# Y W from thirds of the channels, on two halves of the array

## The chip, the cores and the metric

The kernel runs on one core of one Trainium2 chip. The metric is the device time of one execution in microseconds (us), the median over several runs.

## The reference

The input x has 8 batches, 3264 positions and 192 channels. Two operations follow each other.

```python
# 1. causal convolution of 7 taps; the taps of each of 8 heads go through a softmax
w = softmax(weight)                       # [8 heads, 7 taps]
x = sum over k of w[head, k] * x_padded[:, s + k, :]
# 2. spectral mix on 64 modes
X = rfft(x, axis=1)[:, :64]               # Xr, Xi
Yr = Xr w_r - Xi w_i                      # per mode a 192 x 192 matrix
Yi = Xr w_i + Xi w_r
y = irfft(Y, n=S)                         # the other modes are zero
u = x + y
out = u + relu(u @ w_ch)                  # w_ch is 192 x 192, called W below
```

The large inputs are x (20 MB), w_r and w_i (9.4 MB each); the output has 20 MB. All are float32; the kernel works in bfloat16 and accumulates in float32.

## The kernel before, in words

The core has five engines that run side by side, each in the order of its own instructions: TensorE (PE; the profile shows its loads of the stationary operand apart, as PEld), VectorE (DVE), ScalarE (ACT), GpSimd (POOL) and SyncE (SP). POOL issues nearly all DMAs, SP a few. The order on each engine is the order of the program text (a manual schedule); waits between engines are put in by the framework, from the parts of tiles that an instruction reads and writes.

Batches are handled in four pairs q = 0 to 3, positions in tiles t of 128 (25 whole ones and a half). A partition of the tile `xall` is a position; the two batches of a pair lie side by side.

**Convolution stage.** `units` are groups of 4 or 5 position tiles. Per unit, `conv` multiplies with a band matrix on 64 x 64 quarters of the array, and two casts write the result back into `xall`: channels 0 to 95 by ACT (L325) and 96 to 191 by DVE (L327). `dft_unit` accumulates the 64 modes, `xtrans` turns them so that channels lie on the partitions. `c_bank` transposes the convolved x into `cc`, with the channels split in thirds (channel 3p + j lies in partition p of third j). The loads of x (L151) are issued ahead, a few small ones among them by the table `beside`.

**Mix stage.** `load_w` (L428) loads the matrices of four modes per group g; `mix` (L439) multiplies them. The result of two groups, a pair d, is copied by ACT into `ymix` (L452), transposed by `mix_trans` (L459), and copied into `yet` (L466 on DVE, L468 on ACT). In `yet`, the partitions are 96 channels, in two halves t; the cosine and the sine part c lie side by side. `PLAN` spreads the waiting transposes (`some`) over the groups. The last group's second half goes through mix, copy and transposes by itself.

**End stage.** The output of a position tile is x W + (inverse transform of Y W) under the relu, plus the inverse transform of Y, plus x. So three kinds of products go into one accumulator: `c_part` (x W, L496, from `cc` and `wc`, two halves of 64 rows at the same time), `m_part(n, 0)` (L516, from Y W), then ACT's relu in place (`relu`, L547), then `m_part(n, 1)` (from Y), and `finish` (L572): DVE adds x into an output buffer and a DMA writes it. Items n are pairs of tiles, `duos`, in a list; the accumulators `zt` are four, so c_part(n + 4) waits for finish(n). The loop runs so, for each n: m_part(n, 0), relu(n), c_part(n + 1), m_part(n - 1, 1), finish(n - 1).

Y W and Y themselves come out of `zw_part` (L523), once for each pair q: for q = 0 before the loop, for q = 1, 2, 3 as items of the list at places 2, 8 and 11, where it uses the accumulator of its place. Item 14 (`"h"`) is the half tiles of all pairs. `zw_part` multiplies 96 rows (channels) of `yet` with `wm` and `w1`, which hold the two halves of the rows of W with an identity beside them, so that each product gives Y W and part of Y. Its result has four blocks of 96 columns; the inner two are Y W, the outer two Y (`QUARTERS`). `zw_copy` scales it into `zw`: DVE L530, ACT L528.

```python
for t, w in enumerate((wm, w1)):
    for i, r in enumerate(ROWS):
        nc.tensor.matmul(z[r, HD - HD * t:2 * D - HD * t], yet[0:HD, t, 2 * q + i, c, :], w[0:HD, :],
                         start=(t == 0), stop=(t == 1), tile_position=(0, 64 * i), skip_group_check=True)
```

The identities of `wm` and `w1` are made by POOL (L253, L254) between the loads of x, and their W is loaded by `small(0)` and `small(1)` (L227) behind the last matrices. `wc` is loaded by `small(2)` and `small(3)` (L229) among the loads of x.

Of the kernel before, what the change touches and what calls it, by code (L numbers as in the profile page):

```python
# [9 lines left out]
ALU = mybir.AluOpType  # L10
# [3 lines left out]
BF16 = mybir.dt.bfloat16  # L14
# [5 lines left out]
def kernel(  # L20
# [9 lines left out]
    nc = tc.nc  # L30
    B, S, D = x.shape
    H, KK = weight.shape
    MODES = moe_w_r.shape[0]
# [3 lines left out]
    P = 128  # L37
# [15 lines left out]
    def sb(name, shape, dtype, **kw):  # L53
        return pool.tile([P] + shape, dtype, tag=name, name=name, **kw)
# [4 lines left out]
    NW = 4  # L59
# [7 lines left out]
    fsin = sb("fsin", [NT, P], BF16)  # L67
    tabs = (ftab, fsin)

    HD = D // 2  # L70
    yet = sb("yet", [2, B, 2, MODES], BF16)

    mixa = sb("mixa", [3 * 2 * B * MODES], BF16)
    xt = mixa[:, :].rearrange("p (j k m) -> p j k m", j=3, k=2 * B)

    zw = mixa[:, 0:4 * NQ * D].rearrange("p (q c b e) -> p q c b e", q=NQ, c=2, b=4)
    QUARTERS = (slice(1, 3), slice(0, 4, 3))
    band = sb("band", [H, 2 * P], BF16)

    wm = sb("wm", [3 * HD], BF16)  # L80
    w1 = sb("w1", [3 * HD], BF16)
    wc = sb("wc", [3, D], BF16)
    ident = sb("ident", [P], BF16)
    perm = sb("perm", [P], BF16)
    ascale = sb("ascale", [1], F32)
# [136 lines left out]
                                     NT * (2 * g + 1):NT * (2 * g + 2) + 1:NT, 0, :], in_=src)  # L222

    def small(k):
        if k < 2:
            w, c, r = ((wm, 0, slice(HD, D)), (w1, HD, slice(0, HD)))[k]
            nc.gpsimd.dma_start(out=w[0:HD, c:c + D], in_=moe_w_ch[r, :])  # L227
        else:
            nc.gpsimd.dma_start(out=wc[64 * (k - 2):64 * (k - 2) + 64, :, :],  # L229
                                in_=moe_w_ch.rearrange("(p j) d -> p j d", j=3))  # L230

    beside = {3: (load_half, 0, 0), 4: (load_half, 0, 1), 6: (load_half, 1, 0), 7: (load_half, 1, 1),
              12: (small, 2), 15: (small, 3)}

    def load_units(k0, k1):
        for k in range(k0, k1):
# [12 lines left out]
    nc.gpsimd.affine_select(out=perm[:, 64:128], in_=perm[:, 64:128], compare_op=ALU.not_equal, fill=1.0,  # L249
                            base=0, pattern=[[-1, 64]], channel_multiplier=1)  # L250
    load_units(5, 9)
    for w, c in ((wm, D), (w1, 0)):
        nc.gpsimd.memset(w[0:HD, c:c + HD], 0.0)  # L253
        nc.gpsimd.affine_select(out=w[0:HD, c:c + HD], in_=w[0:HD, c:c + HD], compare_op=ALU.not_equal,  # L254
                                fill=1.0, base=0, pattern=[[-1, HD]], channel_multiplier=1)
    nc.gpsimd.memset(ascale[:], 2.0 / S)
    nc.gpsimd.memset(ascale[0:1, :], 1.0 / S)
    nc.gpsimd.memset(ascale[64:65, :], 1.0 / S)
# [8 lines left out]
                                                                  mybir.DependencyReason.DATA),  # L267
                              reason="row tiles take turns on a bank")

    LO, UP = slice(0, 64), slice(64, P)  # L270

    def conv_step(q, t0, n, half, step):

# [133 lines left out]
    for k, u in enumerate(units):  # L407
        conv(*u)
        if k < 2:
            table(*PARTS[k + 1])  # L410
        if waiting:
            xtrans(*waiting.pop(0), 0)
        if k:
            q, t0, n = units[k - 1]
            dft_unit(q, t0, n)
            if t0 + n == NT:
                waiting = [(q, 0), (q, 1)]
            if k > 1:
                some(XJOBS[k], min(NT * q + t0 + n, NT * (NQ - 1)))
# [14 lines left out]
    def mix(g):  # L434
        yp = low[(g // 2) % 2][:, D * (g % 2):D * (g % 2) + D]
        for j in range(3):
            for p4 in range(4):
                m = 4 * g + p4
                nc.tensor.matmul(yp[32 * p4:32 * p4 + 2 * B, :], xt[:, j, :, m],  # L439
                                 wbuf(g)[:, p4, j, :], start=(j == 0), stop=(j == 2),  # L440
                                 tile_position=(0, 32 * p4), skip_group_check=True)
        if g < NW:
            load_w(g + NW + NL)
        elif g >= NW + NL:
            load_w(g + NW)
            if g + NW == NG - 1:

                small(0)
                small(1)

    def mix_copy(d, gs=slice(0, 2)):
        nc.scalar.copy(out=ymix[d % 2][:, gs, :],  # L452
                       in_=low[d % 2][:, 0:2 * D].rearrange("p (g d) -> p g d", g=2)[:, gs, :])

    def mix_trans(d, gs=slice(0, 2)):
        ets = [low[2 + t][:, :].bitcast(BF16)[:, 0:2 * P].rearrange("p (g k) -> p g k", g=2) for t in range(2)]
        for t in range(2):
            for g in range(gs.start, gs.stop):
                nc.tensor.transpose(ets[t][0:HD, g, :], ymix[d % 2][:, g, HD - HD * t:D - HD * t], ident[:])  # L459
        m = slice(8 * d + 4 * gs.start, 8 * d + 4 * gs.stop)  # L460
        for t in range(2):
            dst = yet[0:HD, t, :, :, m].rearrange("p b c m -> p c b m")
            srcv = ets[t][0:HD, gs, :].rearrange("p g (q k) -> p (g q) k", q=4)[:, :, 0:16].rearrange(
                "p m (c b) -> p c b m", c=2)
            if t == 0:
                nc.vector.tensor_copy(out=dst, in_=srcv)  # L466
            else:
                nc.scalar.copy(out=dst, in_=srcv)  # L468
# [7 lines left out]

    ROWS = (LO, UP)

    def c_part(n, ks=(0, 1)):
        duo, zt = items[n]
        if duo[0] == "h":
            for a in range(2):
                for j in range(3):
                    for k in range(2):
                        for i, r in enumerate(ROWS):
                            h = ROWS[i ^ k]
                            nc.tensor.matmul(zt[h, k, D * a:D * a + D], cc[r, 2 * k + a, 3 * NF + j, h], wc[r, j, :],
                                             start=(a == 0 and j == 0), stop=False, skip_group_check=True,  # L490
                                             tile_position=(r.start, h.start))
            return
        for k, (q, t) in enumerate(duo):
            for j in range(3) if k in ks else ():
                for i, r in enumerate(ROWS):
                    nc.tensor.matmul(zt[:, i, D * k:D * k + D], cc[r, q, 3 * t + j, :], wc[r, j, :],  # L496
                                     start=(k == 0 and j == 0), stop=False, skip_group_check=True)

    def m_part(n, which):

        duo, zt = items[n]
        for c in range(2):
            end = which == 1 and c == 1
            if duo[0] == "h":
                for k in range(2):
                    for i, r in enumerate(ROWS):
                        h = ROWS[i ^ k]
                        nc.tensor.matmul(zt[h, k, 0:2 * D], tabs[c][r, NF, 0:HALF], zw[r, 2 * k:2 * k + 2, c, QUARTERS[which], :],
                                         start=False, stop=end, skip_group_check=True,
                                         tile_position=(r.start, h.start))  # L510
                continue
            (q0, t0), (q1, t1) = duo[0], duo[-1]
            parts = [(0, 2, q0, t0)] if t0 == t1 and q0 != q1 else [(k, 1, q, t) for k, (q, t) in enumerate(duo)]
            for k, w, q, t in parts:
                for i, r in enumerate(ROWS):
                    nc.tensor.matmul(zt[:, i, D * k:D * (k + w)], tabs[c][r, t, :], zw[r, q:q + w, c, QUARTERS[which], :],  # L516
                                     start=False, stop=end and k + w == len(duo), skip_group_check=True)

    def zw_part(q, c, z):

        for t, w in enumerate((wm, w1)):
            for i, r in enumerate(ROWS):
                nc.tensor.matmul(z[r, HD - HD * t:2 * D - HD * t], yet[0:HD, t, 2 * q + i, c, :], w[0:HD, :],  # L523
                                 start=(t == 0), stop=(t == 1), tile_position=(0, 64 * i), skip_group_check=True)

    def zw_copy(dst, src, act):
        if act:
            nc.scalar.activation(out=dst, in_=src, func=ACT.Copy, scale=ascale[:, 0:1])  # L528
        else:
            nc.vector.tensor_scalar(out=dst, in0=src, scalar1=ascale[:, 0:1], scalar2=None, op0=ALU.mult)  # L530
# [82 lines left out]
    c_part(0)  # L613
    mix_trans(NG // 2 - 1, slice(1, 2))
    c_part(1, (0,))
    for c in range(2):
        zw_part(0, c, low[2 * c])
    for w in QUARTERS:
        for c in range(2):
            zw_copy(zw[:, 0, c, w, :], low[2 * c][:, 0:2 * D].rearrange("p (b e) -> p b e", b=4)[:, w, :], c)  # L620
    c_part(1, (1,))
    low_stack.close()
    stack, pp = psum_pool("pz1", "right")
# [6 lines left out]
    for n in range(N + 1):  # L630
        if is_duo(n) and duos[n] != ("h",):
            m_part(n, 0)
            relu(n)
        if n + 1 < N and n > 0:
            if is_duo(n + 1):
                c_part(n + 1)
                if duos[n + 1] == ("h",):

                    m_part(n + 1, 0)
                    relu(n + 1)  # L640
            else:
                q, zt = items[n + 1]
                for c in range(2):
                    zw_part(q, c, zt[:, c, :])
                for act, w in enumerate(QUARTERS):
                    zw_copy(zw[:, q, :, w, :], zt[:, :, 0:2 * D].rearrange("p c (b e) -> p c b e", b=4)[:, :, w, :],
                            act)
        if is_duo(n - 1):
            m_part(n - 1, 1)
            finish(n - 1)  # L650
# [30 lines left out]
```

## Time and profile before

| | |
|---|---|
| median of 4 runs | 180.48 us (179.97 to 180.79) |
| the profiled execution | 180.16 us |
| its span, first to last instruction | 178.4 us |
| mean granted clock of TensorE | 0.983 of full |
| busy PE, DVE, ACT, POOL | 146.9, 113.0, 98.2, 100.5 us |
| HBM read, written | 39.40 MB, 20.05 MB |

The profile is of one execution. Times in it count from the first instruction of the span; the execution's own time is 1.76 us longer than the span. Busy time of PE includes the flight of pipelined products, so its busy time is not its full rate. A row of a group gives line, engine, operation, output and inputs with their shapes, the count, and durations; "idle before" names what ended the engine's wait, and "issue" stands for a wait for nothing that the profile shows.

### The profile page before, as it was taken

The numbers are of one execution on the slowest core, as the hardware profiler recorded it, in microseconds if no ns is written. First come the engines' busy times: TensorE is split into PE (matmuls) and PEld (weight loads), VectorE is DVE, ScalarE is ACT, GpSimd is POOL, SyncE is SP. The second block draws the span as 40 slices with busy tenths as digits, with TensorE's granted clock in tenths as the row PEclk, the third lists the DMA queues.
The fourth block names the chain that finished last, engine by engine and source line by source line (L and its number), as shares of the span: only waits on it lengthen the run. The fifth ranks groups of instructions, "written<-read, shape, count | busy, mean of one in ns | idle before, by whom it ended". The sixth has DMA issues, their size and how long they took to land.

```text
span 178.4 us, 6295 instructions
## 1 busy us (share of the span) xinstructions
PE 146.9 (82%) x2736; PEld 108.6 (61%) x2736; DVE 113.0 (63%) x161; ACT 98.2 (55%) x135; POOL 100.5 (56%) x155
## 2 busy tenths in 40 slices
PE   0047879999999998796767769999999999999940
PEld 0033456666666665674655656966778888888820
DVE  1878564766866683444435362695788888888870
ACT  8176645544554735163354555767566777666630
POOL 7999988868855644433336100035354766665770
PEclk9999999999999999789999999999999999999997
DMA  3999999999999999999999970567689899998895
GB/s 43 167 176 188 190 190 189 192 191 194 188 191 191 204 206 207 206 207 206 206 206 206 207 120 4 174 227 281 252 248 364 329 366 354 355 348 352 334 355 192
DMA packets 44331, 40.17 MB, mean 225 GB/s; under 512 B 28800, under 2 KB 40656, under 8 KB 44304
## 3 DMA queue, kind: packets, MB, share of 16 engines
q0 software_dynamic: 41136, 37.59, 105.8%
q1 hardware_dynamic: 3168, 2.19, 4.0%
q8 instruction: 21, 0.34, 0.8%
q14 instruction: 6, 0.05, 0.1%
HBM read 39.40 MB, written 20.05 MB: 333 GB/s over the span
## 4 chain that ended last, share of the span: by engine, by line
DMA 42%; POOL 31%; issue 14%; PE 8%; POOLq 1%; DVE 1%; DVEq 0%
DMA arena<-in_moe_w_i_dram 18%; DMA xall<-in_x_dram 18%; POOL out_dram L580 17%; POOL xall L151 10%; DMA cc<-in_moe_w_i_dram 7%; PE za L516 2%; PE za L496 2%; POOL arena L428 1%; PE zb L516 1%; PE zb L496 1%; POOL xall L221 1%; PE zb L523 1%; DVE arena L572 1%; PE low L439 1%; POOLq L676 0%
## 5 line engine op out<-in xcount | busy, mean ns | idle before, releaser
L580 POOL DMA_DIRECT2D out_dram<-arena x45 | 33.9, 754 | 39.6 <-DVE arena L572 38.6
L151 POOL DMA_DIRECT2D xall<-in_x_dram x48 | 38.6, 812 | 7.0 <-DMA xall<-in_x_dram 4.6
L307 PE MATMUL z<-xall,band 64*64 64x192 bf16 (+3 forms) x816 | 27.4, 264 | 14.5 <-ACT band L195 10.5
L327 DVE CAST xall<-z 128x768 bf16<-128x768 f32 (+1 forms) x24 | 24.5, 1021 | 13.9 <-PE z L307 12.5
L307 PEld LDWEIGHTS <-band 64*64 64x64 bf16 x816 | 18.4, 110 | 22.9 <-ACT band L195 10.9
L325 ACT CAST xall<-z 128x768 bf16<-128x768 f32 (+1 forms) x24 | 20.4, 850 | 20.6 <-PE z L307 19.8
L496 PEld LDWEIGHTS <-cc 64*128 64x128 bf16 x600 | 27.3, 94 | 6.1 <-issue 1.3
L572 DVE TENSOR_TENSOR arena<-za,xall 128x768 f32<-128x768 f32 x26 | 24.7, 956 | 5.3 <-ACT zb L547 2.0
L547 ACT ACTIVATE za<-za 128x768 f32<-128x768 f32 (+1 forms) x27 | 21.0, 783 | 8.5 <-PE za L516 8.4
L572 DVE TENSOR_TENSOR arena<-zb,xall 128x768 f32<-128x768 f32 x23 | 21.9, 956 | 5.0 <-ACT zb L547 1.7
L547 ACT ACTIVATE zb<-zb 128x768 f32<-128x768 f32 (+1 forms) x25 | 19.6, 782 | 9.2 <-PE zb L516 8.9
L333 PE MATMUL low<-xall,ftab 128*128 128x384 bf16 x100 | 22.0, 348 | 0.0
L387 PEld LDWEIGHTS <-xall 128*128 128x128 bf16 x300 | 18.5, 104 | 3.2 <-issue 0.3
L362 DVE COPY cc<-r 128x1024 bf16<-128x1024 bf16 (+1 forms) x16 | 10.2, 670 | 13.7 <-ACT xs L452 6.2
L516 PE MATMUL za<-mixa,ftab 64*128 64x384 bf16 (+1 forms) x120 | 18.2, 304 | 0.0
L516 PE MATMUL za<-mixa,fsin 64*128 64x384 bf16 (+1 forms) x120 | 18.2, 304 | 0.0
L496 PE MATMUL za<-wc,cc 64*128 64x192 bf16 x318 | 18.1, 243 | 0.0
L516 PE MATMUL zb<-mixa,ftab 64*128 64x384 bf16 (+1 forms) x100 | 16.2, 313 | 0.4 <-ACT zb L547 0.4
L516 PE MATMUL zb<-mixa,fsin 64*128 64x384 bf16 (+1 forms) x100 | 16.2, 313 | 0.0
L496 PE MATMUL zb<-wc,cc 64*128 64x192 bf16 x282 | 15.9, 243 | 0.1
L428 POOL DMA_DIRECT2D arena<-in_moe_w_r_dram x12 | 7.4, 615 | 13.7 <-PE low L439 8.5
L516 PEld LDWEIGHTS <-ftab 64*128 64x128 bf16 x220 | 12.0, 94 | 4.2 <-issue 2.0
(110 smaller groups left out, 185.9 us busy)
## 6 DMA issues: line engine op xcount, KB each, us to landing
out_dram<-arena POOLq DMA_DIRECT2D x45, 384.0 KB, 4.3
xall<-in_x_dram POOLq DMA_DIRECT2D x24, 192.0 KB, 7.4
xall<-in_x_dram POOLq DMA_DIRECT2D x16, 240.0 KB, 7.2
arena<-in_moe_w_r_dram POOLq DMA_DIRECT2D x12, 288.0 KB, 9.2
arena<-in_moe_w_i_dram POOLq DMA_DIRECT2D x12, 288.0 KB, 10.0
out_dram<-arena SPq DMA_DIRECT2D x9, 192.0 KB, 2.4
xall<-in_x_dram POOLq DMA_DIRECT2D x8, 144.0 KB, 7.1
cc<-in_moe_w_r_dram POOLq DMA_DIRECT2D x4, 288.0 KB, 11.6
```

What stands on the lines that cost most here:

```text
L151: nc.gpsimd.dma_start(out=xall[:, s0:s0 + nf, i, :], in_=src)
L307: mm = nc.tensor.matmul(ov[c], band[r, h, c.start + shift + 64 * (r is UP and c is LO): c.start + shift + 64 * (r is UP and c is LO) + 64] ...
L325: nc.scalar.copy(out=dst, in_=srcv)
L327: nc.vector.tensor_copy(out=dst, in_=srcv)
L333: nc.tensor.matmul(xp, ftab[:, t, :], xall[:, slot(q, t), :, :], start=(t == 0), stop=False, skip_group_check=True)
L362: nc.vector.tensor_copy(out=out, in_=in_)
L387: nc.tensor.transpose(tp[:, P * k:P * k + P], src, ident[:])
L496: nc.tensor.matmul(zt[:, i, D * k:D * k + D], cc[r, q, 3 * t + j, :], wc[r, j, :], start=(k == 0 and j == 0), stop=False, skip_group_check ...
L516: nc.tensor.matmul(zt[:, i, D * k:D * (k + w)], tabs[c][r, t, :], zw[r, q:q + w, c, QUARTERS[which], :], start=False, stop=end and k + w = ...
L547: nc.scalar.activation(out=zt[:, :, 0:w], in_=zt[:, :, 0:w], func=ACT.Relu)
L572: nc.vector.tensor_tensor(out=o[:, :, :].rearrange("p k (i d) -> p i k d", i=2), in0=zt[:, :, 0:2 * D].rearrange("p i (k d) -> p i k d", k=2),
L580: nc.gpsimd.dma_start(out=dst, in_=ov)
```

## The change

Y W and Y are now made from thirds of the channels. `mix_trans` transposes each third twice, once into partitions 0 to 63 and once into 64 to 127 (12 transposes of 64 columns for a pair, in one bank, in place of 4 of 96 in two). From the lower half DVE takes the cosine part, from the upper half ACT the sine part, so that `yet` has 64 channels of one third on each half. `zw_part` then multiplies the two halves of the array side by side, three products each, of 384, 320 and 256 columns, for both batches of the pair at once.

The moving operand is `wc`, as in the c products, widened by an identity for each third; `wm`, `w1`, their POOL instructions and their two loads go. The identity columns of `wc` are written by DVE, one memset and three additions, after the fourth unit of the convolution. Y comes out in the order of thirds, and the copy into `zw` puts it back in order. For pairs 2 and 3 both copies run on ACT; for pairs 0 and 1 they stay with DVE and ACT.

```diff
-    yet = sb("yet", [2, B, 2, MODES], BF16)
+    yet = sb("yet", [3, B, MODES], BF16)
...
-    wm = sb("wm", [3 * HD], BF16)
-    w1 = sb("w1", [3 * HD], BF16)
-    wc = sb("wc", [3, D], BF16)
+    wc = sb("wc", [3, 2 * D], BF16)
...
     def small(k):
-        if k < 2:
-            w, c, r = ((wm, 0, slice(HD, D)), (w1, HD, slice(0, HD)))[k]
-            nc.gpsimd.dma_start(out=w[0:HD, c:c + D], in_=moe_w_ch[r, :])
-        else:
-            nc.gpsimd.dma_start(out=wc[64 * (k - 2):64 * (k - 2) + 64, :, :],
-                                in_=moe_w_ch.rearrange("(p j) d -> p j d", j=3))
+        nc.gpsimd.dma_start(out=wc[64 * k:64 * k + 64, :, 0:D], in_=moe_w_ch.rearrange("(p j) d -> p j d", j=3))
...
-    for w, c in ((wm, D), (w1, 0)):
-        nc.gpsimd.memset(w[0:HD, c:c + HD], 0.0)
-        nc.gpsimd.affine_select(out=w[0:HD, c:c + HD], in_=w[0:HD, c:c + HD], compare_op=ALU.not_equal,
-                                fill=1.0, base=0, pattern=[[-1, HD]], channel_multiplier=1)
...
+        if k == 3:
+            nc.vector.memset(wc[:, :, D:2 * D], 0.0)
+            for j in range(3):
+                nc.vector.tensor_tensor(out=wc[:, j, D + 64 * j:D + 64 * j + 64], in0=ident[:, 0:64],
+                                        in1=ident[:, 64:P], op=ALU.add)
...
-            if g + NW == NG - 1:
-
-                small(0)
-                small(1)
...
     def mix_trans(d, gs=slice(0, 2)):
-        ets = [low[2 + t][:, :].bitcast(BF16)[:, 0:2 * P].rearrange("p (g k) -> p g k", g=2) for t in range(2)]
-        for t in range(2):
-            for g in range(gs.start, gs.stop):
-                nc.tensor.transpose(ets[t][0:HD, g, :], ymix[d % 2][:, g, HD - HD * t:D - HD * t], ident[:])
+        ets = low[2 + d % 2][:, :].bitcast(BF16)[:, 0:6 * P].rearrange("p (j g k) -> p j g k", j=3, g=2)
+        for g in range(gs.start, gs.stop):
+            yv = ymix[d % 2][:, g, :].rearrange("k (p j) -> k j p", j=3)
+            for j in range(3):
+                for r in ROWS:
+                    nc.tensor.transpose(ets[r, j, g, :], yv[:, j, :], ident[:], tile_position=(0, r.start))
...
+        for c, r in enumerate(ROWS):
+            dst = yet[r, :, :, m]
+            srcv = ets[r, :, gs, :].rearrange("p j g (q k) -> p j (g q) k", q=4)[:, :, :, B * c:B * c + B].rearrange(
+                "p j m b -> p j b m")
+            if c == 0:
                 nc.vector.tensor_copy(out=dst, in_=srcv)
             else:
                 nc.scalar.copy(out=dst, in_=srcv)
...
-    def zw_part(q, c, z):
...
+    def zw_part(q, zs):
+        for j in (2, 1, 0):
+            n = D + 64 * (j + 1)
+            for r, z in zip(ROWS, zs):
+                nc.tensor.matmul(z[:, 0:n], yet[r, j, 2 * q:2 * q + 2, :], wc[r, j, 0:n],
+                                 start=(j == 2), stop=(j == 0), skip_group_check=True)
+
+    def zw_views(q, cs, z, w):
+        dst, src = zw[:, q, cs, w, :], z[:, :, D * w:D * w + D]
+        if w:
+            dst, src = dst.rearrange("p c (e j) -> p c e j", j=3), src.rearrange("p c (j e) -> p c e j", j=3)
+        return dst, src
...
-    for c in range(2):
-        zw_part(0, c, low[2 * c])
-    for w in QUARTERS:
+    zw_part(0, (low[0], low[2]))
+    for w in range(2):
         for c in range(2):
-            zw_copy(zw[:, 0, c, w, :], low[2 * c][:, 0:2 * D].rearrange("p (b e) -> p b e", b=4)[:, w, :], c)
+            zw_copy(*zw_views(0, slice(c, c + 1), low[2 * c][:, :].unsqueeze(1), w), c)
...
-                for c in range(2):
-                    zw_part(q, c, zt[:, c, :])
-                for act, w in enumerate(QUARTERS):
-                    zw_copy(zw[:, q, :, w, :], zt[:, :, 0:2 * D].rearrange("p c (b e) -> p c b e", b=4)[:, :, w, :],
-                            act)
+                zw_part(q, (zt[:, 0, :], zt[:, 1, :]))
+                for w in range(2):
+                    zw_copy(*zw_views(q, slice(0, 2), zt, w), w if q == 1 else 1)
```

More of the change, by code (lines that the diff above doesn't have):

```diff
@@ L68 @@
     tabs = (ftab, fsin)
-    HD = D // 2
-    yet = sb("yet", [2, B, 2, MODES], BF16)
+    yet = sb("yet", [3, B, MODES], BF16)
     mixa = sb("mixa", [3 * 2 * B * MODES], BF16)
     xt = mixa[:, :].rearrange("p (j k m) -> p j k m", j=3, k=2 * B)
-    zw = mixa[:, 0:4 * NQ * D].rearrange("p (q c b e) -> p q c b e", q=NQ, c=2, b=4)
-    QUARTERS = (slice(1, 3), slice(0, 4, 3))
+    zw = mixa[:, 0:4 * NQ * D].rearrange("p (q c t d) -> p q c t d", q=NQ, c=2, t=2)
     band = sb("band", [H, 2 * P], BF16)
-    wm = sb("wm", [3 * HD], BF16)
-    w1 = sb("w1", [3 * HD], BF16)
-    wc = sb("wc", [3, D], BF16)
+    wc = sb("wc", [3, 2 * D], BF16)
     ident = sb("ident", [P], BF16)
@@ L224, in small @@
     def small(k):
-        if k < 2:
-            w, c, r = ((wm, 0, slice(HD, D)), (w1, HD, slice(0, HD)))[k]
-            nc.gpsimd.dma_start(out=w[0:HD, c:c + D], in_=moe_w_ch[r, :])
-        else:
-            nc.gpsimd.dma_start(out=wc[64 * (k - 2):64 * (k - 2) + 64, :, :],
-                                in_=moe_w_ch.rearrange("(p j) d -> p j d", j=3))
+        nc.gpsimd.dma_start(out=wc[64 * k:64 * k + 64, :, 0:D], in_=moe_w_ch.rearrange("(p j) d -> p j d", j=3))
     beside = {3: (load_half, 0, 0), 4: (load_half, 0, 1), 6: (load_half, 1, 0), 7: (load_half, 1, 1),
-              12: (small, 2), 15: (small, 3)}
+              12: (small, 0), 15: (small, 1)}
     def load_units(k0, k1):
@@ L268, in turn @@
                               reason="row tiles take turns on a bank")
-    LO, UP = slice(0, 64), slice(64, P)
+    ROWS = LO, UP = slice(0, 64), slice(64, P)
     def conv_step(q, t0, n, half, step):
@@ L455, in mix_trans @@
     def mix_trans(d, gs=slice(0, 2)):
-        ets = [low[2 + t][:, :].bitcast(BF16)[:, 0:2 * P].rearrange("p (g k) -> p g k", g=2) for t in range(2)]
-        for t in range(2):
-            for g in range(gs.start, gs.stop):
-                nc.tensor.transpose(ets[t][0:HD, g, :], ymix[d % 2][:, g, HD - HD * t:D - HD * t], ident[:])
-        m = slice(8 * d + 4 * gs.start, 8 * d + 4 * gs.stop)
[L461 to L465, printed above, removed]
+        ets = low[2 + d % 2][:, :].bitcast(BF16)[:, 0:6 * P].rearrange("p (j g k) -> p j g k", j=3, g=2)
[4 more added lines that the diff above has]
+                    nc.tensor.transpose(ets[r, j, g, :], yv[:, j, :], ident[:], tile_position=(0, r.start))
+        m = slice(8 * d + 4 * gs.start, 8 * d + 4 * gs.stop)
+        for c, r in enumerate(ROWS):
[3 more added lines that the diff above has]
+            if c == 0:
                 nc.vector.tensor_copy(out=dst, in_=srcv)
@@ L475 @@
     tjobs = [(0, g_bank, c, t0, min(8, NT - t0)) for c in (1, 0) for t0 in range(0, NT, 8)] + tjobs
-    ROWS = (LO, UP)
     def c_part(n, ks=(0, 1)):
@@ L488, in c_part @@
                             h = ROWS[i ^ k]
-                            nc.tensor.matmul(zt[h, k, D * a:D * a + D], cc[r, 2 * k + a, 3 * NF + j, h], wc[r, j, :],
+                            nc.tensor.matmul(zt[h, k, D * a:D * a + D], cc[r, 2 * k + a, 3 * NF + j, h], wc[r, j, 0:D],
                                              start=(a == 0 and j == 0), stop=False, skip_group_check=True,
@@ L495, in c_part @@
                 for i, r in enumerate(ROWS):
-                    nc.tensor.matmul(zt[:, i, D * k:D * k + D], cc[r, q, 3 * t + j, :], wc[r, j, :],
+                    nc.tensor.matmul(zt[:, i, D * k:D * k + D], cc[r, q, 3 * t + j, :], wc[r, j, 0:D],
                                      start=(k == 0 and j == 0), stop=False, skip_group_check=True)
@@ L507, in m_part @@
                         h = ROWS[i ^ k]
-                        nc.tensor.matmul(zt[h, k, 0:2 * D], tabs[c][r, NF, 0:HALF], zw[r, 2 * k:2 * k + 2, c, QUARTERS[which], :],
+                        nc.tensor.matmul(zt[h, k, 0:2 * D], tabs[c][r, NF, 0:HALF], zw[r, 2 * k:2 * k + 2, c, which, :],
                                          start=False, stop=end, skip_group_check=True,
@@ L515, in m_part @@
                 for i, r in enumerate(ROWS):
-                    nc.tensor.matmul(zt[:, i, D * k:D * (k + w)], tabs[c][r, t, :], zw[r, q:q + w, c, QUARTERS[which], :],
+                    nc.tensor.matmul(zt[:, i, D * k:D * (k + w)], tabs[c][r, t, :], zw[r, q:q + w, c, which, :],
                                      start=False, stop=end and k + w == len(duo), skip_group_check=True)
-    def zw_part(q, c, z):
[L521 to L524, printed above, removed]
+    def zw_part(q, zs):
[9 more added lines that the diff above has]
+        return dst, src
     def zw_copy(dst, src, act):
```

## The prediction

> **What bounds the kernel now.** I read the busy time by stage first, to see which engine has no slack where.
>
> ```profile
> 70.00:80.00 10.00, 8.26 (x182) 6.21 (x182) 3.95 (x8) 4.31 (x8) 3.66 (x6) 0.83 1.21 206
> 100.00:105.00 5.00, 3.31 (x67) 2.72 (x65) 2.32 (x5) 2.91 (x5) 0.00 (x0) 1.00 1.15 191
> 110.00:115.00 5.00, 5.00 (x107) 4.33 (x103) 2.57 (x4) 3.82 (x6) 0.00 (x0) 1.00 0.29 94
> 140.00:150.00 10.00, 10.00 (x180) 8.32 (x178) 8.31 (x10) 6.85 (x10) 6.72 (x10) 1.00 0.95 360
> ```
>
> Columns: length, busy PE, PEld, DVE, ACT, POOL, then granted clock, DMA share, GB/s. Until 105 the DMA engines are full and PE has gaps; from 110 PE has none. The chain of waits puts the border at the last weights:
>
> ```profile
> 96.97 10.04 DMA arena<-in_moe_w_i_dram
> 107.01 0.04 issue
> 107.06 0.46 PE low L439 x12
> ...
> 117.29 0.61 PE za L523 x8
> ...
> 120.48 0.61 PE zb L523 x8
> ```
>
> So the end is: last landing (107.0), a serial passage of about 3 us through copies, transposes and the first Y W, then PE's work without gaps to 171.5. The products that change (L523, four groups of 8) lie in the last two parts. The timeline of the serial passage, weight loads and DVE:
>
> ```profile
> 108.64 0.39 PEld L523 LDWEIGHTS <-yet 96*64 96x64 bf16 x8 [0.16 <-DVE yet L466]
> 109.25 0.20 PEld L496 LDWEIGHTS <-cc 64*128 64x128 bf16 x6 [0.22 <-issue]
> ...
> 109.23 0.74 DVE L530 TENSOR_SCALAR mixa<-low,ascale 128x192 bf16<-128x192 f32 x2 [0.66 <-PE low L523]
> ```
>
> And of a later group, weight loads and DVE:
>
> ```profile
> 117.22 0.39 PEld L523 LDWEIGHTS <-yet 96*64 96x64 bf16 x8 [0.32 <-issue]
> 117.83 0.10 PEld L516 LDWEIGHTS <-ftab 64*128 64x128 bf16 x2 [0.23 <-issue]
> 119.48 0.44 PEld L496 LDWEIGHTS <-cc 64*128 64x128 bf16 x11 [0.23 <-issue]
> ...
> 117.06 0.96 DVE L572 TENSOR_TENSOR arena<-za,xall 128x768 f32<-128x768 f32 x1 [0.19 <-ACT zb L547]
> 118.48 1.81 DVE L572 TENSOR_TENSOR arena<-zb,xall 128x768 f32<-128x768 f32 x2
> ```
>
> PE stands before and after each L523 group with nothing to wait for, and DVE's additions (L572), which free the buffers for the c products three items later, end just before those products start.
>
> **The change part by part.** Times are those of the profiled execution: span 178.4, its own time 180.16 (1.76 outside the span); the median of the runs is 180.48, 0.32 above it.
>
> *Loading, to 107.0.* Two loads of w_ch (36 KB each, issued at 97.57 and 98.67, behind the last weights) and four POOL instructions at 20.90 to 21.94 go. The loads lie behind the landing that counts, and the queue ran at 191 GB/s over 20 to 24 in spite of the POOL work: 0. The two loads into wc stay, cut into pieces of 384 B written instead of 1152 B. Pieces like the first ran at 191 GB/s (x, 30 to 50), like the second at 206 (weights, 60 to 100); 147 KB takes 0.77 us instead of 0.71: +0.06.
>
> *DVE in the convolution stage.* One memset and three additions of 64 columns after the cast that ends at 26.04. Nearest rows: memset of 128x152, 185 ns; addition 128x56 bf16, 216 ns; so 0.7 to 1.1 us. Cover: PE's gaps before the weight groups, 0.6 to 1.1 us each from 84 on, swallow a late convolution several times over. Taken at 0; 1.1 if the cover is gone.
>
> *Mix stage, seven and a half pairs.* Per pair 12 transposes of 64 columns for 4 of 96, and copies of 64 partitions x 192 for 96 x 128. The 64-column pairs of L346/L348 start 0.05 to 0.09 apart, so 0.3 to 0.4 us for 0.25; copies go from 283 to about 350 ns (DVE) and 264 to about 320 (ACT), on the slope between the 64- and 128-element rows (216 to 283, 210 to 264). Same gaps, cost 0.
>
> *Serial passage.* The last half pair has no cover. Six transposes instead of two end 0.05 later; copies of 96 elements instead of 64 last 0.03 longer; with the pipeline between, the first Y W starts at 108.75, +0.11. It is now three pairs of products, lower and upper half together, of 384, 320 and 256 columns. A 384-column pair of the same 64-row shape takes 0.163 (L516 starts 116.63, 116.79, 116.95), so 0.163 + 0.136 + 0.109 = 0.41 against four pairs in 0.61 on the chain. But formerly the cosine half was ready first (109.08, the sine half 109.33) and DVE copied early; now both end together at about 109.32 (start of the last pair 109.05, its flight 0.27). DVE starts at 109.44 instead of 109.23, the first product with its result at 109.91 instead of 109.70. The second half waited until 109.89 for ACT before too, so the block of four ends at 110.56 instead of 110.38: +0.18.
>
> *Second group (110.49).* PE is done 0.3 us earlier, but what follows, m_part(0,1), needs the relu of item 0, which ACT ran from 110.33 to 111.08 and now runs to about 111.26: start 111.32 instead of 111.17. Next, c_part(4) started at 112.81 on the end of DVE's addition of item 0 (112.72); that is +0.11. Gain of this group: lost.
>
> *Third group (117.22).* From the last start before it (116.95 + 0.163) to the next product at 117.84 PE spends 0.73; now 0.41: -0.31. Half of that is no gain: c_part(9) started at 118.17, 0.15 after DVE's addition of item 5 ended (118.02); that addition is 0.11 late, so the start is 118.18. c_part(10) waited for the addition of item 6 until 119.48 (the pause of 0.23); that now ends at 119.19 and PE arrives at 119.33. Offset here: -0.15.
>
> *Fourth group (120.41).* -0.31 again, offset -0.46. c_part(13) at 122.15 for 122.67 (addition of item 9), c_part of the half tiles at 123.16 for 123.59 (addition of item 10): -0.43. After that the items repeat every 1.15 us with PE full, and the offset stays.
>
> *Copies of two pairs on ScalarE.* DVE loses 2 x 0.62, ACT gains 2 x 0.58. ACT used to wait for DVE here (L528 0.53 idle, twice), so its queue moves little: relu(9), queued behind, starts at 119.58, when its product ends, and m_part(9,1) needs it at 120.56. Reading every 64th column is not in the trace. Bounds: the same 0.58 (contiguous 384 take 0.48 without the scale), or twice that, which would make relu(9) 0.4 late and eat 0.3. I take the low end, since the casts of L327, which write in pieces of 24, take as long as the contiguous additions of that size (0.953 and 0.956).
>
> Sum: -0.43 + 0.06 = -0.37; 180.16 becomes 179.8, the median 180.48 becomes **180.1**.
>
> [...]
>
> **The rivals.**
>
> *More is kept (faster).* The passage at 108 is not longer and the additions do not hold c_part(9): the third and fourth groups bring 0.31 each, the removed pauses before c_part(10) and (13) 0.15 more: -0.77 + 0.06, 179.8; with the second group's 0.3 too, 179.5. For: DVE is idle for 2.4 of the 5 us from 110 to 115. Against: m_part(0,1) at 111.17 lies 0.09 behind the relu. Chance 0.39.
>
> *No gain.* The upper and lower products do not run side by side, so a group costs 0.82 and not 0.41: about 180.5. Against: the 12 products of L496 take 0.49, six pairs of 0.08. Or the copies cost double: 180.4. Chance 0.08.
>
> *The half clock moves (slower).* The granted clock was 0.83 over 70 to 80: 3.4 us at half. There PE had gaps. If such a stretch falls behind 107, where PE has none, it costs half of 3.4, 1.7 us, less the gain: 181.8. It decides as soon as 0.5 us of it lie behind 107 more than the gain covers. For: the new order shifts PE's work between 70 and 107. Against: it adds work there, and the clock is 1.00 in all stages from 80 to 170. Chance 0.09.
>
> *The new memset waits for the loads into wc (slower).* They are issued earlier in the program and land at about 44; DVE would stand from 26 to 44, the mix would start near 90 instead of 73, the queue would run dry (loads land some 10 us after their issue), and the end would come 7 us or more later: about 188. Against: the casts of L325 (24.82 to 25.62) and L327 (25.08 to 26.04) write interleaved halves of the same rows without waiting for each other, and wc's parts are just as interleaved. Chance 0.03.
>
> **How the numbers follow.** About 0.3%, 0.54 us, is what a measurement of this kernel can tell from no change. The forecast, 0.38, and "no gain", 0.08, give 0.46 for within 0.3%. "More is kept" gives faster, 0.39. Slower: 0.09 + 0.03, and 0.03 for a load that ends late: 0.15. Range 179.3 to 181.0: below, 179.5 and 0.2 for the landing; above, the doubled copies (180.4), the 0.3 by which the highest run lies over the median, and 0.3 of DVE's work uncovered. It leaves out the last two rivals and some of the low tail.
>
> **What would show it.** Right: the new products as six of 64 rows per group, no pause of 0.2 to 0.3 around the last three; first of them near 108.75; c_part(9) bound by DVE; last weights still at 107.0 to 107.1; PE's last product near 171.1. Wrong: a landing moved by over 0.3, a clock below 1.00 after 107, an ACT copy over 0.8 us, DVE idle on a DMA at 26.

## The result and the profile after

The changed kernel takes 181.11 us (median of 36 runs, 179.71 to 183.07) against 180.38 of the kernel before (55 runs beside it): 1.0034 times, interval 1.0019 to 1.0049. The ratio is that of the means and leaves out the one slow run, 183.07. The forecast was 180.1, and 181.0 was the upper end of the range. The profiled execution took 181.57 (span 179.7). All ratios below are to the kernel before, run beside it on the same chip; the experiments ran on four chips.

**The stages.** The same windows, with the columns of before:

```profile
70.00:80.00 10.00, 7.59 (x191) 5.69 (x185) 4.69 (x8) 4.47 (x7) 3.67 (x6) 1.00 1.21 207
100.00:105.00 5.00, 3.58 (x75) 2.91 (x72) 2.93 (x5) 2.70 (x4) 0.00 (x0) 1.00 1.11 188
110.00:115.00 5.00, 4.56 (x98) 3.91 (x94) 3.18 (x5) 3.76 (x7) 0.00 (x0) 1.00 0.09 30
140.00:150.00 10.00, 10.00 (x178) 7.65 (x176) 8.31 (x10) 6.85 (x10) 6.71 (x10) 1.00 0.96 362
```

The half clock of 70 to 80 (0.50 for 3.4 us) lies at 20 to 30 in this profile (0.83 there), and the clock is 1.00 in every window from 70 to 170. Over 110 to 115 PE has gaps of 0.44 now.

**The serial passage,** first in the chain of waits:

```profile
97.08 10.42 DMA arena<-in_moe_w_i_dram
107.50 0.04 issue
107.54 0.46 PE low L430 x12
...
109.02 0.26 DVE yet L455
...
109.33 0.73 PE low L512 x4
...
110.18 0.42 DVE mixa L526
```

The last weights land at 107.50 instead of 107.01. Next, the timeline of ACT in the same passage:

```profile
109.30 0.23 ACT L457 COPY yet<-low 64x96 bf16<-64x96 bf16 x1 [0.93 <-DVE yet L455]
...
111.25 0.80 ACT L543 ACTIVATE za<-za 128x768 f32<-128x768 f32 x1 [0.26 <-PE za L503]
```

And the one of weight loads, down to the fourth group:

```profile
109.32 0.09 PEld L512 LDWEIGHTS <-yet 64*128 64x128 bf16 x1 [0.29 <-DVE yet L455]
109.59 0.12 PEld L512 LDWEIGHTS <-yet 64*128 64x128 bf16 x4 [0.17 <-ACT yet L457]
...
117.86 0.44 PEld L512 LDWEIGHTS <-yet 64*128 64x128 bf16 x6
118.32 0.11 PEld L503 LDWEIGHTS <-ftab 64*128 64x128 bf16 x2
...
118.98 0.44 PEld L483 LDWEIGHTS <-cc 64*128 64x128 bf16 x11 [0.29 <-issue]
...
121.08 0.27 PEld L512 LDWEIGHTS <-yet 64*128 64x128 bf16 x5 [0.21 <-issue]
```

ACT's copy of the sine part waits for DVE's copy of the cosine part, which is no input of it: the two copies run one after the other. Further down the third group (117.86) has no pause before or behind it, but c_part(9) (118.98) has one of 0.29, and the fourth group (121.08) stands too. DVE's additions say for what:

```profile
117.97 0.96 DVE L568 TENSOR_TENSOR arena<-za,xall 128x768 f32<-128x768 f32 x1 [0.19 <-ACT zb L543]
119.04 1.99 DVE L568 TENSOR_TENSOR arena<-zb,xall 128x768 f32<-128x768 f32 x2
...
171.85 0.55 DVE L563 TENSOR_TENSOR arena<-za,xall 128x384 f32<-128x384 f32 x1
173.85 0.56 DVE L563 TENSOR_TENSOR arena<-zb,xall 128x384 f32<-128x384 f32 x1 [1.45 <-DMA out_dram<-arena]
```

The additions end at 118.93 and 121.03, each 0.05 before the weight load that stood. The last two rows are the end of the kernel: the last addition waits 1.45 for its output buffer, that is, for the landing of an older output. Before, these two additions followed each other directly:

```profile
171.60 0.55 DVE L567 TENSOR_TENSOR arena<-za,xall 128x384 f32<-128x384 f32 x1
172.07 0.55 DVE L567 TENSOR_TENSOR arena<-zb,xall 128x384 f32<-128x384 f32 x1
```

The first of the two comes 0.25 later than before, the last output, as shown next, 1.56 later: most of the loss in this profile arises in the outputs and not in PE's work. The windows of the last microseconds, before:

```profile
172.00:175.00 3.00, 0.00 (x0) 0.00 (x0) 0.62 (x2) 0.00 (x0) 1.43 (x2) 1.00 0.98 369
...
177.00:178.00 1.00, 0.00 (x0) 0.00 (x0) 0.00 (x0) 0.00 (x0) 0.00 (x0) 0.50 0.00 0
```

and after:

```profile
172.00:175.00 3.00, 0.00 (x0) 0.00 (x0) 0.95 (x2) 0.00 (x0) 1.47 (x3) 1.00 0.96 361
...
177.00:178.00 1.00, 0.00 (x0) 0.00 (x0) 0.00 (x0) 0.00 (x0) 0.00 (x0) 0.50 0.06 21
178.00:179.00 1.00, 0.00 (x0) 0.00 (x0) 0.00 (x0) 0.00 (x0) 0.00 (x0) 0.50 0.02 5
```

The DMA share (last column but one) is 0.00 behind 177 before; after, it is 0.06 for a further microsecond, which is one of 16 DMA engines. The last output lands at 178.66 instead of 177.10. One engine is late with its part of the outputs: in the trace's packets, all others have finished the output that SP issues by 176.77, the last one at 178.26. What could hold one engine up stands in the instructions of each engine and the queue table of the page (packets, MB, share). Before:

```profile
PE 146.9 (82%) x2736; PEld 108.6 (61%) x2736; DVE 113.0 (63%) x161; ACT 98.2 (55%) x135; POOL 100.5 (56%) x155
...
q8 instruction: 21, 0.34, 0.8%
```

After:

```profile
PE 146.5 (82%) x2792; PEld 106.8 (59%) x2792; DVE 113.9 (63%) x163; ACT 100.2 (56%) x137; POOL 98.7 (55%) x149
...
q8 instruction: 22, 0.36, 0.8%
```

The queue q8 brings TensorE's program, in packets of 16 KB: 21 of them go with the 5472 products and weight loads of before, 22 with the 5584 of after, and between the first packet and the last 5085 and 5329 of them start, 254 to a packet: taken here as 256, an estimate from these counts that b_pad256, below, bears out. The change has 56 more matmuls and, with the weight load of each, 112 more instructions, so 22 packets instead of 21, and those behind the new instructions come at other times. In the trace's packets the last two of before began at 159.5 and 166.2; of after at 163.3 and 170.5, and this one took 1.6 us on its engine, in the middle of the last outputs.

### The profile page after: what moved, and what is told of

It is laid out like the page before. It is cut to its first block, busy times and chain, and to the rows that moved or that the text cites. A ratio compares the mean times of both kernels' runs of the same rounds, so it can differ in the third digit from the quotient of the medians.

```text
span 179.7 us, 6398 instructions
## 1 busy us (share of the span) xinstructions
PE 146.5 (82%) x2792; PEld 106.8 (59%) x2792; DVE 113.9 (63%) x163; ACT 100.2 (56%) x137; POOL 98.7 (55%) x149
## 4 chain that ended last, share of the span: by engine, by line
DMA 45%; POOL 28%; issue 12%; PE 8%; DVE 2%; ACT 1%; POOLq 0%; DVEq 0%; ACTq 0%
DMA arena<-in_moe_w_i_dram 18%; DMA xall<-in_x_dram 18%; POOL out_dram L576 14%; POOL xall L146 10%; DMA cc<-in_moe_w_i_dram 7%; DMA out_dram<-arena 3%; PE za L503 2%; PE za L483 2%; POOL arena L419 1%; PE zb L503 1%; DVE arena L568 1%; POOL xall L216 1%; PE zb L483 1%; PE low L430 1%; PE low L512 0%
## 5 line engine op out<-in xcount | busy, mean ns | idle before, releaser
L483 PEld LDWEIGHTS <-cc 64*128 64x128 bf16 x600 | 26.6, 94 | 6.7 <-issue 0.9
L503 PE MATMUL za<-mixa,ftab 64*128 64x384 bf16 (+1 forms) x120 | 17.7, 304 | 0.4 <-DVE mixa L526 0.2
L503 PE MATMUL za<-mixa,fsin 64*128 64x384 bf16 (+1 forms) x120 | 17.7, 304 | 0.0
L503 PE MATMUL zb<-mixa,ftab 64*128 64x384 bf16 (+1 forms) x100 | 15.6, 313 | 0.4 <-ACT zb L543 0.4
L503 PE MATMUL zb<-mixa,fsin 64*128 64x384 bf16 (+1 forms) x100 | 15.7, 313 | 0.0
L346 ACT COPY cc<-r 128x1024 bf16<-128x1024 bf16 (+1 forms) x9 | 8.9, 989 | 9.5 <-PE r L373 8.4
```

## The experiments

My theory from here: the packet at 170.5 makes one DMA engine late, and this is most of the loss; a smaller part is the one bank of the new transposes. Rivals: it is the serial passage and PE alone; or ACT, which now copies alone for pairs 2 and 3; or the wait for the output buffer, as such.

**The program's length alone.** The kernel before with products at the start that nothing reads (they run from 0.99 to 4.2 us, when PE has no other work), each a weight load and a matmul. Only their number differs:

```diff
+    zpad = sb("zpad", [64], BF16)
+    nc.vector.memset(zpad[:], 0.0)
+    for _ in range(56):       # b_pad112; 28 in b_pad56, 88 in b_pad176, 128 in b_pad256
+        nc.tensor.matmul(low[3][0:64, 0:64], zpad[:, 0:64], zpad[:, 0:64], start=True, stop=True, skip_group_check=True)
```

> The kernel before, with 56 products of zeros (112 PE instructions, weight loads included) ahead of the convolution, where PE has nothing to do: the PE program is then exactly as long as the changed one (5586 instead of 5474). Theory A, fetches: TensorE's program comes in pieces of 16 KB (256 instructions) over the same DMA engines as the data, and the place of these pieces decides: pieces near 106 and 170 as in the changed kernel, last weights land near 107.5 instead of 107.0, the last addition waits for its output buffer; 180.7 to 181.2, 0.2 to 0.4% slower than before. Theory B, serial passage: the length of the program is of no account, 180.4 plus or minus 0.2.

Measured: 1.0028 [1.0009, 1.0047], with a program as long as the changed kernel's and nothing else of the change. Its last two packets began at 162.3 and 170.4 (1.7 us). Its page:

```profile
PE 150.0 (83%) x2792; PEld 109.5 (61%) x2792; DVE 113.3 (63%) x162; ACT 98.2 (55%) x135; POOL 100.6 (56%) x155
...
q8 instruction: 22, 0.36, 0.8%
```

DVE's timeline at its end:

```profile
171.59 0.55 DVE L572 TENSOR_TENSOR arena<-za,xall 128x384 f32<-128x384 f32 x1
173.93 0.56 DVE L572 TENSOR_TENSOR arena<-zb,xall 128x384 f32<-128x384 f32 x1 [1.79 <-DMA out_dram<-arena]
```

Its windows behind 177:

```profile
177.00:178.00 1.00, 0.00 (x0) 0.00 (x0) 0.00 (x0) 0.00 (x0) 0.00 (x0) 0.50 0.06 23
178.00:179.00 1.00, 0.00 (x0) 0.00 (x0) 0.00 (x0) 0.00 (x0) 0.00 (x0) 0.50 0.02 8
```

The same wait, the same single engine behind 177, the last landing at 178.75. One output shows where it sets in (times of issue and landing): before 167.84 to 171.94, with these products 167.82 to 173.81, in the changed kernel 168.08 to 173.72; the outputs issued just before take 4 us in all three. So the slow end can be had without any of the change's work. That the last weights would land late as well was expected and did not happen: they landed at 107.19, in spite of a packet at 105.0.

Other lengths put the packets elsewhere:

> The kernel before with 128 products of zeros at the start: 256 PE instructions, one whole piece, so all later pieces begin at the same places of the work as before. Theory A in the form that the place decides: as before, 180.4 plus or minus 0.2, last fetch near 166, the last addition does not wait. In the form that every piece costs: at least as slow as with 112 (180.9) or slower.

> The kernel before with 28 products of zeros (56 instructions). Theory A by place: the piece that came at 108.0 comes near 106.5, into the last weights, landing 107.3 to 108; the last piece comes near 164 and a new one near 172, after the buffer of the last addition was freed or just at it: 180.6 to 181.2. Theory that only the sum of instructions counts, in proportion: 180.65.

> The kernel before with 88 products of zeros (176 instructions). Theory A by place: pieces near 103 and 168; the tail is free as in the run with 144, the last addition starts about 172; 180.4 to 180.6. By number: 180.9 as with 112.

> The kernel before with 56 instructions of padding, as measure for the three beside it on the same chip: 0.9984 as in its first run, 180.0 to 180.3.

b_pad256 adds a whole packet, so that the last ones come at 159.1 and 166.2 as in the kernel before: 1.0009 [0.9988, 1.003]. b_pad56 (last at 165.4 and 164.0 in its two profiles): 0.9984 [0.9965, 1.0004] and 0.9986 [0.9962, 1.001]; a further packet near 172 and a loss had been expected of it, and there was neither. The place fits these times and the number does not, though the intervals of 256 and 112 overlap. b_pad176 has its last packet at 168.0, its last landing at 177.59, and 1.0035 [1.0004, 1.0066] is wide. By its interval this can be scatter; its trace says that a packet at 168 costs as well.

The traces show why the place matters. A packet holds up the outputs wherever it falls in the end stage, in the kernel before too: there the outputs that POOL issues land about 1.0 us apart, but 2.0 to 3.0 us behind the packets at 137.2, 145.0, 151.7, 159.5 and 166.2 comes one gap of 2.09, 2.28, 1.82, 1.85 and 1.73. Over all 18 profiles, 79 of the 86 packets between 136 and 171.5 are followed by a gap of 1.5 or more within 4.2 us, and 79 of the 88 such gaps from 136 on follow a packet.

What differs is what comes behind. Items come every 1.15 us and late outputs land 0.98 apart, so about 0.17 per item is made good (an estimate from these rows): a gap of 1.73 is worked off after four or five items, while one of 2.72, as behind 170.5 in the changed kernel, would take ten, and only six outputs are left. So no sharp moment is to be expected from which a packet harms. The single late engine shows in the output that SP issues, 256 packets of 768 bytes and 16 of 4 bytes, a sixteenth for each of the profile's 16 engines (an estimate from these counts; in the changed kernel 16 and 1 of them begin behind 177, one after the other): with a last packet at 168.0 or later (eight profiles), the last engine ends 0.55 to 1.96 behind the last but one, 0.99 in b_pad176; with an earlier one (ten profiles) 0.03 to 0.57.

**The changed kernel with its packets elsewhere.** The same products, 72, 64 and 96 of them, at its start:

> The changed kernel, with 72 products of zeros (144 PE instructions) at the start: together with its own 112 more this is one whole piece of 256, so the pieces begin at the same places of the later work as before the change. Theory A, fetches: no piece in the last 6 us, the last addition does not wait for a buffer, 180.3 to 180.7, though one piece more is fetched in all. Theory B: 181.1 as the changed kernel, the passage from last weights to first item still 0.46 longer than before.

> The changed kernel with 128 PE instructions of padding, the place at which its two-bank form measured 0.9995 of before. If the change by itself costs (one bank, passage 0.4 longer): 180.6 to 180.9. If all of its loss was the place: 180.1 to 180.4. By the prediction's sum it would be 0.4 faster than before, 180.0.

> The changed kernel with 192 instructions of padding: together with its own the place of the kernel before with 56, which measured 0.9984. Change costs: 180.5 to 180.8. Place was all: 180.0 to 180.3.

Last packets at 167.7, 166.9 and 164.9; measured 1.0016 [0.9995, 1.0037], 1.0017 [0.9995, 1.0039] and 0.9998 [0.9969, 1.0027]. The change with no packet behind 168 is at the kernel before or 0.1 to 0.2% behind it, and nowhere ahead by anything that could be told. The three profiled executions still end late, at 178.34, 178.11 and 178.17 (b_pad256: 177.89), but with most DMA engines and not with one: the last products start at 172.67, 172.01 and 172.06 (171.86), before at 171.44. The time of the last landing alone therefore does not sort the kernels.

**One bank or two.** Back to two banks, one for each destination half, in the changed kernel:

```diff
-        ets = low[2 + d % 2][:, :].bitcast(BF16)...
+        ets = [low[2 + c][:, :].bitcast(BF16)... for c in range(2)]
...
-                for r in ROWS:
-                    nc.tensor.transpose(ets[r, j, g, :], ...)
+                for c, r in enumerate(ROWS):
+                    nc.tensor.transpose(ets[c][r, j, g, :], ...)
```

> The changed kernel, with the transposes of the two halves in two banks instead of one; as many instructions. Theory B, serial passage: ACT's copy of the sine part waited for DVE's of the cosine part because both read one bank (0.28 us); now they start together, the first products with Y W begin 0.2 to 0.3 earlier after the last weights, and 0.1 to 0.3 of that reaches the end: 180.8 to 181.0. Theory A, fetches: this shift is lost behind the DMAs of the output, 181.1 plus or minus 0.1.

ACT's timeline, to be laid beside the one of after, and DVE's copy:

```profile
108.76 0.23 ACT L457 COPY yet<-low 64x96 bf16<-64x96 bf16 x1 [0.60 <-PE low L448]
...
110.82 0.80 ACT L543 ACTIVATE za<-za 128x768 f32<-128x768 f32 x1 [0.36 <-PE za L503]
...
108.73 0.25 DVE L455 COPY yet<-low 64x96 bf16<-64x96 bf16 x1 [1.73 <-PE low L448]
```

ACT's copy now waits for its transposes and starts 0.03 behind DVE's. From the last landing to relu(0) it is 3.54 us; 3.75 with one bank, 3.32 before. So the bank costs 0.21, and what was priced in the prediction (+0.18) is 0.22. Its time, 1.0007 [0.9989, 1.0026], lies below the changed kernel's (the intervals overlap), though a packet still comes at 171.2 (a short one, 0.9). Two banks together with harmless places:

> The changed kernel with two banks for the transposes and 64 products of zeros (128 instructions) at the start, which puts the pieces near 108 (behind the last weights) and 168. Theory A and B together: no collision with the last weights or the last buffers, passage 0.2 shorter: 180.0 to 180.5, the best of the changed kernels. If fetches do not matter: 180.8 as with two banks alone.

> The two-bank form with 192 instructions of padding: passage 0.2 shorter than in the run with one bank beside it, so 0.1 to 0.2 faster than that one; the candidate to beat both kernels, 179.9 to 180.2.

0.9995 [0.997, 1.002], last packet at 166.2, last landing 176.96; and 0.9998 [0.9974, 1.0022], 164.3 and 177.20. This is the best form of the change, and it cannot be told from the kernel before. One of DVE's additions in a_banks_pad192 shows one way in which PE's lead is lost:

```profile
146.15 1.89 DVE L573 TENSOR_TENSOR arena<-zb,xall 128x768 f32<-128x768 f32 x2 [0.74 <-DMA out_dram<-arena]
```

A packet at 142.7 is followed by a gap of 2.54 between two landings, up to 146.03, and the next addition, at 146.15, has waited 0.74 for its output buffer.

**The copies on ScalarE.** The split between DVE and ACT kept for all pairs:

```diff
-                    zw_copy(*zw_views(q, slice(0, 2), zt, w), w if q == 1 else 1)
+                    zw_copy(*zw_views(q, slice(0, 2), zt, w), w)
```

> The changed kernel, with the copies of pairs 2 and 3 shared between DVE and ACT as before. If two copies on ACT hold the relus back (theory C), this is faster by 0.1 to 0.4. By the working of the prediction, DVE's additions of items 6 and 10 come 0.1 to 0.3 later and the end with them: 0 to 0.2 slower, 181.1 to 181.3.

1.0037 [1.0017, 1.0057], the same as with both copies on ACT (1.0034). These copies take 0.57 to 0.58 each on ACT in the changed kernel, as the ones of before did on ACT (0.58); reading every 64th column costs nothing here, and where they run makes no difference that shows.

**The wait for the output buffer.** The last item gets the buffer of the half tiles (it lies in the tile `band` and is free by then), so that its addition has nothing to wait for:

```diff
+    buffers[-1] = NO
```

> The kernel before, where the last item writes into the buffer of the half tiles (free since about 132) instead of one of the six in turn. Its last addition did not wait in the profile, so nothing is to be had: 180.1 to 180.4. If the buffers held it in most executions, 0.3 faster or more.

> The kernel before with 112 PE instructions more at the start and the last item in its own buffer. If the last addition's wait of 1.8 us for its buffer is what the longer program costs, the time falls from 180.9 to 180.2 to 180.5. If the delay lies in the landing of the last output itself, whatever buffer, it stays at 180.7 to 181.0.

> The changed kernel with the last item in its own buffer: the same question for it. Wait decides: 180.3 to 180.7. Landing decides: 181.0.

> The changed kernel with two banks for the transposes and the last item in its own buffer: both repairs, 179.9 to 180.4 if the wait decides, 180.5 to 180.8 if the landing does.

In the longer kernel before, the wait is gone:

```profile
171.55 0.55 DVE L574 TENSOR_TENSOR arena<-za,xall 128x384 f32<-128x384 f32 x1
172.02 0.55 DVE L574 TENSOR_TENSOR band<-zb,xall 128x384 f32<-128x384 f32 x1
```

and the time isn't: 1.0049 [1.0024, 1.0074], last landing 178.49. Likewise in the changed kernel (addition at 172.06, last landing 178.14, 1.0066 [1.0041, 1.0092]) and with two banks (1.0035 [1.001, 1.0061], 178.54). In the kernel before, which has no such wait, the buffer does nothing: 0.9986 [0.9961, 1.0011]. The wait is a symptom. The late engine decides, whether DVE waits for it or not.

**All runs in one table,** by where the last packet began:

| | packet at 170 to 171.2 | last packet at 168 or earlier |
|---|---|---|
| kernel before and additions | 1.0028, 1.0049 | 0.9984, 0.9986, 0.9986, 1.0009, 1.0035 (at 168.0) |
| change, one bank | 1.0034, 1.0037, 1.0066 | 1.0017, 1.0016, 0.9998 |
| change, two banks | 1.0007, 1.0035 | 0.9995, 0.9998 |

By the means of the rows, with 168.0 counted on the right, the packet costs 0.25 to 0.4%. One bank against two, in the four pairs of kernels alike otherwise (not all run on one chip), costs 0.27, 0.31, 0.22 and 0.00%, 0.2% in the mean, against 0.21 us (0.12%) in the traces. Single intervals are as wide as these differences; the table carries them by agreement, the two-banks row least.

## Why the prediction was wrong

**The step that failed: "cost 0 in mix stage" for the new transposes.** The prediction looked for their price beside PE's gaps, and there they are hidden indeed. It counted their time and not their instructions. Twelve transposes for four per pair make 64 more matmuls, the Y W groups are 8 fewer: 56 more in all. The program got longer by 112 instructions, and its last packets moved from 159.5 and 166.2 to 163.3 and 170.5. That is a transfer on the resource that sets the end of the kernel: over 172 to 175 the DMA engines are busy for 0.98 of the time. None of the rivals had it; the range fell short by 0.1 us. The packets in the trace of before and the number of new instructions would have given it: the last packets of before are 6.7 us apart, so 112 of 256 instructions bring the same packet 2.9 us forward, from 166.2 to 163.3, where it was found, and the next one, 6.7 behind it, to 170.0 (found at 170.5), while PE runs until 171.7. PE itself did not stand for such a packet: over 140 to 150, with one at 148.6, it is busy for 10.00 of 10 us. The outputs are held up, and the measured 1.0028 of b_pad112 decides.

**Serial passage: +0.18, measured +0.43.** The priced part was right (+0.22 with two banks). The missing 0.21 is the order of two copies out of one bank. The prediction had both copies at once, though the profile of before shows a wait of this kind (L528, 0.53 idle behind DVE), which it used for the copies of Y W and didn't carry over to the one bank of the new transposes. The two copies lie in partitions 0 to 63 and 64 to 127 of the bank. Whether the wait has to be, or is only put in by the framework, was not shown: in no run do the two copies read one bank together.

**Second group: right.** PE was done earlier, and m_part(0,1) still waited for the relu (112.10).

**Third group: right.** The last pair before it starts at 117.85; with its 0.163 and up to the next product at 118.42 it is 0.41, as predicted, and the two pauses are gone, so they didn't belong to the group as such. That they would go was assumed in both terms of -0.31, and no run had shown it. What the traces show is where such pauses stand: 0.32 and 0.23 around the old group (weight loads of 96x64 among 64x128), 0.32 and 0.30 before and behind the half tiles (64x64) in both kernels (weight loads at 124.01 and 124.96, before at 123.59 and 124.54), and none around the new third group, 64x128 like its neighbours. c_part(9) then starts 0.05 behind the end of the addition, as said.

**Fourth group: predicted -0.31, got -0.17** (0.71 instead of 0.88 from the last product before it to the next one behind it). The group itself uses an accumulator, the one of item 7, whose addition ended only at 121.03; the group started at 121.08. The prediction followed the additions to the c products and not to this group. By then PE was ahead of DVE, and what it gained it spent waiting.

**The sum.** Measured from the last landing, c_part of the half tiles is 0.07 earlier than before, where 0.43 was expected; 0.21 of the gap is the bank, 0.14 the fourth group. "The offset stays" failed too, as far as the end goes: against the kernel before with a program of the same length (1.0028), the change (1.0034) is no faster, and even with two banks and its packets elsewhere it is at 0.9995 and 0.9998; one place where a lead is lost is the wait for an output buffer shown for a_banks_pad192. From the forecast's -0.37 to the +0.61 measured (by the means) it is 0.98 us: the packet is 0.50 by b_pad112, PE's smaller gain 0.36, and the rest is within the intervals. The landing itself was 0.49 late in this profile; over the profiles of all kernels here, before and after mixed, it lies between 106.41 and 108.11, so this is no effect that one profile can show.

**Smaller terms.** DVE's memset and additions took 0.30 and 0.40, 0.70 at 26.04 to 26.84, right after the cast and with no wait for a DMA; the lower bound was right, and so was the cover, since PE still waited 0.80 for the last weights at 107.54 (0.70 before):

```profile
26.04 0.30 DVE L398 MEMSET wc<- 128x288 uint32 x1
...
26.44 0.40 DVE L400 TENSOR_TENSOR wc<-ident 128x64 bf16<-128x64 bf16 x3
```

The copies on ACT took the low end (1.04 for two). Of the rivals, the half clock, the wait of the memset and products that don't run side by side are refuted by these rows; "more is kept" failed on the additions, which hold c_part(9) and the fourth group.

## What to carry to other kernels

Count the instructions that an edit adds or removes on each engine, also where their time is hidden, and look where the fetches of that engine's program fall: at the end of a kernel that waits for its outputs, one of them shifted the result by 0.28% here (b_pad112). For a comparison of this fineness, run the old kernel with its program made as long as the new one's; only against that is the rest of the change measured. Before putting two engines' sources into one bank, look for a wait between readers of one bank in the trace, and when a stage gets shorter, ask for every accumulator behind it, the stage's own too, when it comes free.

## What the runs showed of the hardware

A fetch of 16 KB of TensorE's program took 0.9 to 2.0 us on one DMA engine while outputs ran, and 79 of 86 were followed by a gap of 1.5 us or more between two landings of outputs, which otherwise came about 1.0 apart. At 170.4 us of a kernel that ends near 178 it put the last landing from 177.10 to 178.75, 1.65 later and so about the fetch's own length of 1.7, with only 1 of 16 engines busy behind 177. That the late engine is the one that made the fetch is argued from this (the trace doesn't tell the engines apart). The profiles show 1.6 us of it and the means 0.5 to 0.9 (b_pad112 1.0028, b_pad112_lastbuf 1.0049). The profiled execution of b_pad112 is 0.67 above its median, that of before 0.22 below its own; why the cost differs from run to run is open.
